# Attention stage of a three-stage kernel: one partial sum on GpSimd instead of two on TensorE, and a new order of sums, masks, hashes and weight splits

## The chip, the cores and the metric

The kernel runs on one core of a Trainium2 chip. The metric is the device time of one execution in microseconds, the median of three runs. The profile is one further execution, recorded by the hardware profiler.

## The reference

Three stages run one after the other: an attention whose mask comes from a hash, a dense layer with a gated activation and a normalisation, and a mixture of eight experts. The change touches the first stage, and the conversion of the second stage's weights, which is done during the first.

```python
def _attn_ref(q, k, v, proj):            # q, k, v: 2 x 8 heads x 768 x 64, float32
    q_bits = (einsum('bhsd,dk->bhsk', q, proj) > 0)   # 6 bits for each row
    k_bits = (einsum('bhsd,dk->bhsk', k, proj) > 0)
    mask = q_bucket[:, :, :, None] == k_bucket[:, :, None, :]
    scores = scale * matmul(q, k.T)
    scores = where(mask, scores, -1e9)
    scores = scores - max(scores, axis=-1)
    attn = exp(scores)
    attn = attn / (sum(attn, axis=-1) + 1e-09)
    return matmul(attn, v)
```

`moe_w_in` and `moe_w_out` arrive as float64, so that the kernel has to build float32 values from two 32-bit words by integer operations before it can use them.

## The kernel before

**Tiling.** The 16 heads are worked on as eight pairs j = 0..7, the two heads of a pair on partitions 0 to 63 and 64 to 127. The 768 queries of a pair are two halves i = 0, 1 of 384; the 768 keys are six blocks c = 0..5 of 128. `run` is an order written out by hand: for each half there are six steps c, each with one `score(j, i, c)` and zero to two `rowmax` calls that are nine ahead in their own list (`scan`), so that the row maxima of pair j+1 begin in the middle of pair j. After step c = 1 the function `first(j)` (for i = 0) or `second(j)` (for i = 1) is called, and it does everything else: AV of the half before, masks, hash, conversions, evacuation, sums. The reader can think of a half as a burst of scores and row maxima with a block of other TensorE work in it after step 1.

**A score.** `both` (line 220) issues four jobs of two matmuls, one for each head, in float32r: high times high, high times low, low times high, and the mask product. The result lies in a "wide" PSUM tile of two banks (`ps`, three buffers). ScalarE writes its exponential to one of eight SBUF tiles `pt` (line 260). A `rowmax` is two jobs into the same kind of PSUM tile; VectorE reduces it (line 236). So scores and row maxima share one ring of three tiles, and each tile comes free when ScalarE or VectorE has read it.

**Sums.** GpSimd adds the exponentials of two blocks each time c is odd (line 264); at c = 3 it also adds the first partial sum to the second (line 266). Two partial sums are left, one of c = 0..3 and one of c = 4, 5. `total` (line 289) adds them over partitions with a matmul by ones on TensorE in float32, into the single PSUM bank `pm`; VectorE copies the result with a small constant to `rb` (line 301). `sums` is called right after AV in `first` and `second`. For i = 1 it also sends `rb` by DMA into a small tile `rc`; `recip` (line 310), called at step c = 4 of the next pair's first half, takes the reciprocal and sends it through DRAM (`rd`) back to all partitions, and `norm` (line 321), called in `first` of the pair after, multiplies.

**AV.** `av` (line 269) is float32, twelve matmuls by the program, each of which the trace shows as two. `evac` (line 280) copies one column by VectorE (`vb`) and then the result by ScalarE.

**Masks and hash.** `hash` (line 191) is four small float32 matmuls and a VectorE threshold; `mask` (line 208) is four bfloat16 matmuls into two wide tiles and two ScalarE copies. `turn` (line 165) makes the high part of q and k on ScalarE and the low part on GpSimd.

**Weights.** The generator `Weights.steps` hands out sixteen conversions, one for each half. `convert()` in `run` calls all operations of one at once: `join` is one ScalarE and three VectorE operations in the bank `pm`; for the first eight (`w_in`) ScalarE then makes the high part and GpSimd the low part from the SBUF tile `w`, for the last eight (`w_out`) ScalarE scales in place.

**Queues.** Loads of q, k and v, the DMAs of `mr`, `rc`, `rd` and the clearing of the scratch rows (`clear`, line 1165, one of 1 MB in each of the first seven `second(j)`) all go through SP's queue in program order.

Of the kernel before, what the change touches and what calls it, by code (L numbers as in the profile page):

```python
# [8 lines left out]
F32 = mybir.dt.float32  # L9
F32R = mybir.dt.float32r  # L10
BF16 = mybir.dt.bfloat16
AF = mybir.ActivationFunctionType
ALU = mybir.AluOpType
# [3 lines left out]
P = 128  # L17
# [8 lines left out]
HW = S // 2  # L26
# [7 lines left out]
I32 = mybir.dt.int32  # L34
# [84 lines left out]
class Attention:  # L119
# [31 lines left out]
    def bank(self):  # L151
        return self.pm.tile([P, 512], F32, tag="pm", name="pm")
# [12 lines left out]
    def turn(self, j):  # L165
        nc, st = self.nc, self.st[j]
        if j == 0:
            self.hash(0)
        for nm in "qk":
            hi, lo = (self.op.tile([P, 2, HW], F32R, tag=x + nm, name=x + nm) for x in ("H", "L"))  # L170
            (nc.vector.tensor_copy if (j, nm) == (0, "q") else nc.scalar.copy)(hi, st["T" + nm])
            if (j, nm) == (0, "k"):
                self.threshold(0)
            eng = nc.gpsimd if j else nc.vector
            eng.tensor_tensor(out=lo, in0=st["T" + nm], in1=hi.bitcast(F32), op=ALU.subtract)
            st["H" + nm], st["L" + nm] = (x.rearrange("p i n -> p (i n)") for x in (hi, lo))

    def warm(self, n):
        ps = self.narrow()[:, 0:P]
# [70 lines left out]
    def score(self, j, i, c):  # L250
        nc, st = self.nc, self.st[j]
        pt = st["pt", i, c] = self.pt[self.npt % NPT]
        self.npt += 1
        ps = self.wide()
        k, q = slice(c * P, (c + 1) * P), slice(i * HW, (i + 1) * HW)
        self.both(
            ps,
            [(st[w][:, k], st[x][:, q]) for w, x in (("Hk", "Hq"), ("Hk", "Lq"), ("Lk", "Hq"), ("Fk", "Fq"))],
        )
        nc.scalar.activation(out=pt[:, :, 0:HW], in_=ps, func=AF.Exp, scale=0.125)  # L260
        if c % 2:
            acc = self.ap.tile([P, 2, HW], F32, tag="acc", name="acc", bufs=4)
            parts = st.setdefault(("acc", i), [])
            nc.gpsimd.tensor_tensor(out=acc, in0=st["pt", i, c - 1][:, :, 0:HW], in1=pt[:, :, 0:HW], op=ALU.add)  # L264
            if c == 3 and (j, i) != self.last:
                nc.gpsimd.tensor_tensor(out=acc, in0=parts.pop(), in1=acc, op=ALU.add)
            parts.append(acc)

# [11 lines left out]
    def evac(self, j, i):  # L280
        nc, st = self.nc, self.st[j]
        x = st["x", i]
        vb = self.sp.tile([P, 1], F32, tag="vb", name="vb")
        nc.vector.tensor_copy(vb, x[:, HW:HW + 1])
        if i == 0:
            st["xr"] = self.ap.tile([P, 2, HW], F32, tag="xr", name="xr", bufs=2)
        nc.scalar.activation(out=st["xr"][:, i], in_=x[:, 0:HW], func=AF.Identity, bias=vb, scale=1.0)
# [47 lines left out]
    def run(self, n, extra, fills):  # L335
        self.last = (n - 1, 1)
        scan = [(j, i, c, kh) for j in range(n) for i in range(2) for c in range(3) for kh in range(2)]

        def scans(m):
            for x in scan[:m]:  # L340
                self.rowmax(*x)
            del scan[:m]

        self.mask(0)
        next(extra)
        for _ in range(NC):
            scans(1)
            self.warm(1)
        self.submax(0, 0)
        self.load(0, "v")  # L350
        self.load(1, "v")
        for _ in range(3):
            scans(1)
            self.warm(1)
        half = [tuple(range(NC)), (0, 1, 2), (3, 4, 5)]

        def convert():
            for f in next(extra, []):
                f()

        def first(j):
            self.submax(j, 1)
            if j + 1 < n:
                self.turn(j + 1)
                self.hash(j + 1)
            convert()
            if j:
                self.av(j - 1, 1, half[0])
            if j > 1:
                self.norm(j - 2)  # L370
            if j + 1 < n:
                self.mask(j + 1)
            if j:
                self.evac(j - 1, 1)
                self.sums(j - 1, 1)
                if j + 1 < n:
                    self.load(j + 1, "v")
            if j + 2 < n:
                self.load(j + 2, "qk")

        def second(j):
            if j + 1 < n:
                self.submax(j + 1, 0)
            convert()
            self.av(j, 0, half[0])
            self.evac(j, 0)
            if j + 1 < n:
                self.sums(j, 0)
            if fills:
                fills.pop(0)()  # L390

        for j in range(n):
            for i in range(2):
                for c in range(NC):
                    self.score(j, i, c)
                    scans(((2, 1, 0, 1, 1, 1), (2, 1, 1, 1, 1, 0))[i][c])
                    if c == 1:
                        (second if i else first)(j)
                    if j and (i, c) == (0, 4):
                        self.recip(j - 1)  # L400
                    if (j, i) == self.last:
                        if c == 2:
                            self.direct(j, 0)
                            self.norm(j - 1)
                        if c == 4:
                            self.av(j, 1, half[1])
        self.av(n - 1, 1, half[2])
        self.evac(n - 1, 1)
        self.direct(n - 1, 1)
        for ops in extra:  # L410
            for f in ops:
                f()


class Weights:
# [10 lines left out]
    def steps(self, pool, bank):  # L426
        nc = self.nc
        todo = [(0, k, h) for k in range(4) for h in range(2)] + [(1, f, 0) for f in range(8)]
        wide = self.src[0].dtype != F32
# [21 lines left out]
        def convert(n):  # L451
            m, k, h = todo[n]
            w = got[n]
            ops = []
            if wide:
                H, L = w[:, :, 1], w[:, :, 0]
                w = self.wo[:, k, :] if m else pool.tile([P, 512], F32, tag="w", name="w", bufs=2)
                wi = w.bitcast(I32)
                V = nc.vector

                def join():
                    a = bank()
                    ai = a.bitcast(I32)
                    nc.scalar.activation(out=a, in_=H.bitcast(F32), func=AF.Copy, scale=2.0 ** -112)
                    V.tensor_scalar(
                        out=ai, in0=ai, scalar1=4, scalar2=1, op0=ALU.logical_shift_left, op1=ALU.logical_shift_right
                    )
                    V.scalar_tensor_tensor(
                        out=ai, in0=L, scalar=29, in1=ai, op0=ALU.logical_shift_right, op1=ALU.bitwise_or
                    )  # L470
                    V.scalar_tensor_tensor(
                        out=wi, in0=H, scalar=-(1 << 31), in1=ai, op0=ALU.bitwise_and, op1=ALU.bitwise_or
                    )

                ops = [join]
            if m:
                ops.append(lambda: nc.scalar.activation(out=w, in_=w, func=AF.Copy, scale=self.g[:, k:k + 1]))
            else:
                hi, lo = (x[:, k, h * 512:h * 512 + 512] for x in self.wi)
                ops += [  # L480
                    lambda: nc.scalar.copy(hi, w),
                    lambda: nc.gpsimd.tensor_tensor(out=lo, in0=w, in1=hi.bitcast(F32), op=ALU.subtract),
                ]
            return ops
# [3 lines left out]
        for n in range(len(todo)):  # L488
            ops = convert(n)
# [22 lines left out]
class Ffn:  # L512
# [33 lines left out]
    def split(self, i):  # L546
        nc = self.nc
        b, c = divmod(i, NC)
        st = self.st[i] = {}
        src = self.xT[:, b, :, c * P:(c + 1) * P]  # L550
        st["xh"] = self.xp.tile([P, 4, P], F32R, tag="xh", name="xh")
        st["xl"] = self.xp.tile([P, 4, P], F32R, tag="xl", name="xl")
        nc.scalar.copy(st["xh"], src)  # L553
        self.sub(nc.gpsimd, st["xl"], src, st["xh"])
# [364 lines left out]
class Experts:  # L919
# [134 lines left out]
    def finish(self, e, t):  # L1054
        nc, st = self.nc, self.st[e]
        y = self.rp.tile([P, DM], F32, tag="y", name="y")
        r = st["r"][t][:, DM:DM + 1]
        nc.vector.tensor_scalar(out=y, in0=st["o"][t], scalar1=r, scalar2=None, op0=ALU.mult)
        ins = nc.gpsimd.indirect_dma_start(
            out=self.out, out_offset=bass.IndirectOffsetOnAxis(ap=st["id"][t][:, 0:1], axis=0), in_=y, in_offset=None,  # L1060
            bounds_check=N - 1, oob_is_err=False,
        )
        apart(self.tc, "out", ins, self.C["gap"])
# [181 lines left out]
```

## Time and profile before

| | us |
|---|---|
| median of three runs | 623.01 (621.53 to 623.53) |
| the profiled execution | 620.83 |
| its span, first to last instruction of the program | 619.1 |
| TensorE busy in the span | 594.8 (96%) |
| VectorE, ScalarE, GpSimd busy | 394.1, 271.7, 317.2 |
| granted TensorE clock, mean | 0.991 |

The attention stage takes the first 248.6 us of the span, the dense layer follows to about 412 us, the experts fill the rest. Times in all rows are microseconds from the start of the span, unless a row says ns. PE is TensorE's matmul, PEld its weight load, DVE VectorE, ACT ScalarE, POOL GpSimd, SP the engine that issues most DMAs; a name with q behind it is the engine's queue. A matmul on PE is shown as busy also while it drains, so the distance from one start to the next tells more than the duration.

### The profile page before, as it was taken

To read this page: it belongs to the slowest core of one execution; us is meant where nothing else is said; L and a number is where in the kernel's file an instruction comes from. 1 tells how busy PE (TensorE), PEld (TensorE's weight loads), DVE (VectorE), ACT (ScalarE), POOL (GpSimd) and SP (SyncE) were. 2 spreads that over 40 slices of the span, in tenths; PEclk is the share of its full clock that TensorE was granted. 3 is DMA by queue.
4 is the path that set the end of the run, shared out by engine and by line. 5 is a ranking of instruction groups with operands and counts; after the bars stand their busy time and mean duration, and the time that the engine had idled before them with its cause. 6 is when DMAs were issued, how large, how long until landed. Compare 5 with 4: busy or idle time off the path is not lost.

```text
span 619.1 us, 10113 instructions
## 1 busy us (share of the span) xinstructions
PE 594.8 (96%) x3910; PEld 460.8 (74%) x3910; DVE 394.1 (64%) x788; ACT 271.7 (44%) x449; POOL 317.2 (51%) x261
## 2 busy tenths in 40 slices
PE   7979999999999999799999999989999999999994
PEld 4656666666666675578888888868899899899893
DVE  5566676767776764886777876573746645636620
ACT  2065555656555655423323322343554454553520
POOL 1076786867676546900110122052967758758731
PEclk9999999999999999989999999989999999999998
DMA  3224546163545422500000002036494494597200
GB/s 125 63 87 136 137 108 199 46 202 113 135 131 139 121 70 95 204 1 1 0 2 1 0 38 51 0 121 239 139 323 164 179 321 149 190 317 247 70 20 34
DMA packets 46229, 72.95 MB, mean 118 GB/s; under 512 B 11227, under 2 KB 20187, under 8 KB 46174
## 3 DMA queue, kind: packets, MB, share of 16 engines
q1 hardware_dynamic: 41326, 57.13, 29.3%
q10 hardware_dynamic: 2608, 8.79, 4.4%
q0 software_dynamic: 2240, 6.31, 2.9%
q8 instruction: 32, 0.52, 0.4%
q14 instruction: 23, 0.19, 0.1%
HBM read 58.39 MB, written 14.78 MB: 118 GB/s over the span
## 4 chain that ended last, share of the span: by engine, by line
PE 90%; ACT 3%; DVE 3%; issue 1%; DMA 1%; POOL 0%; POOLq 0%; SPq 0%; ACTq 0%; DVEq 0%
PE ps L224 18%; PE g L1021 15%; PE o L1043 14%; PE x L275 10%; PE h L562 10%; PE y L562 10%; PE pm L295 4%; ACT pt L260 2%; PE pm L181 2%; PE t L625 2%; PE x L988 1%; PE ps L213 1%; PE ps L195 1%; PE t L652 1%; PE lg L677 1%
## 5 line engine op out<-in xcount | busy, mean ns | idle before, releaser
L961 POOL TENSOR_TENSOR wl<-ws,wh 128x512 fp32r<-128x512 f32 x75 | 107.3, 1464 | 53.6 <-ACT wh L959 53.6
L264 POOL TENSOR_TENSOR acc<-pt,pt 128x768 f32<-128x768 f32 x48 | 87.8, 1838 | 85.5 <-ACT pt L260 85.4
L236 DVE TENSOR_REDUCE m<-ps 128x2 f32<-128x768 f32 x96 | 90.5, 957 | 43.5 <-PE ps L224 42.2
L260 ACT ACTIVATE pt<-ps 128x768 f32<-128x768 f32 x96 | 76.2, 814 | 68.2 <-PE ps L224 68.1
L959 ACT CAST wh<-ws 128x512 fp32r<-128x512 f32 x128 | 70.3, 617 | 5.2 <-POOL wl L961 3.5
L275 PE MATMUL x<-pt,v 128*64 128x385 f32 x384 | 65.8, 491 | 0.0
L961 DVE TENSOR_TENSOR wl<-ws,wh 128x512 fp32r<-128x512 f32 x53 | 57.9, 1125 | 10.3 <-ACT wh L959 10.1
L1027 DVE SCALAR_TENSOR_TENSOR hl<-g,hh 128x512 fp32r<-128x512 f32 x32 | 22.1, 692 | 59.8 <-ACT hh L1026 59.8
L538 POOL TENSOR_TENSOR xl<-xT,xh 128x512 fp32r<-128x512 f32 x12 | 16.1, 1344 | 82.4 <-ACT xh L553 38.5
L1026 ACT ACTIVATE hh<-g 128x512 fp32r<-128x512 f32 x32 | 19.2, 599 | 81.5 <-PE g L1021 81.5
L562 PE MATMUL h<-wi,xh 128*128 128x512 f32 x192 | 50.8, 408 | 3.8 <-DVE e L590 3.8
L275 PEld LDWEIGHTS x<-pt,v 128*64 128x64 f32 x384 | 26.1, 137 | 34.4 <-issue 34.0
L1043 PE MATMUL o<-wh,hh 128*128 128x512 f32 x128 | 51.1, 399 | 0.0
L1043 PE MATMUL o<-wh,hl 128*128 128x512 f32 x128 | 50.5, 394 | 0.0
L1043 PE MATMUL o<-wl,hh 128*128 128x512 f32 x128 | 50.5, 394 | 0.0
L562 PEld LDWEIGHTS h<-wi,xh 128*128 128x128 f32 x192 | 35.8, 194 | 11.9 <-issue 4.2
L562 PE MATMUL y<-wo,lh 128*128 128x512 f32 x176 | 42.7, 394 | 0.0
L224 PE MATMUL ps<-Hq,Hk 64*128 64x384 f32 x192 | 38.6, 398 | 3.1 <-ACT Fk L217 2.5
L1021 PE MATMUL g<-xh,wh 128*128 128x256 f32 x256 | 41.3, 283 | 0.3 <-ACT xh L990 0.2
L224 PE MATMUL ps<-Hk,Hq 64*128 64x384 f32 x192 | 41.5, 429 | 0.0
L1021 PE MATMUL g<-xl,wh 128*128 128x256 f32 x256 | 41.2, 282 | 0.0
L1021 PE MATMUL g<-xh,wl 128*128 128x256 f32 x256 | 40.8, 282 | 0.0
(226 smaller groups left out, 1197.0 us busy)
## 6 DMA issues: line engine op xcount, KB each, us to landing
ws<-in_moe_w_dram SPq DMA_DIRECT2D x32, 1024.0 KB, 9.8
scratch<-zero SPq DMA_DIRECT2D x7, 1030.0 KB, 7.5
r<-scratch SPq DMA_DIRECT2D x16, 257.5 KB, 4.0
raw<-in_moe_w_in_dram ACTq DMA_DIRECT2D x8, 512.0 KB, 4.0
raw<-in_moe_w_out_dram ACTq DMA_DIRECT2D x8, 512.0 KB, 4.3
q<-in_q_dram SPq DMA_DIRECT2D x8, 384.0 KB, 4.6
v<-in_v_dram SPq DMA_DIRECT2D x8, 384.0 KB, 3.0
k<-in_k_dram SPq DMA_DIRECT2D x7, 384.0 KB, 4.5
```

The lines of the kernel that those rows point to most:

```text
L224: self.nc.tensor.matmul(ps[:, h], w[r], x[r], start=(n == 0), stop=(n == len(jobs) - 1), tile_position=(D * h, 0))
L236: nc.vector.tensor_reduce(out=st["m", i][:, c, :, kh], in_=ps, axis=AX.X, op=ALU.max, negate=True)
L260: nc.scalar.activation(out=pt[:, :, 0:HW], in_=ps, func=AF.Exp, scale=0.125)
L264: nc.gpsimd.tensor_tensor(out=acc, in0=st["pt", i, c - 1][:, :, 0:HW], in1=pt[:, :, 0:HW], op=ALU.add)
L275: nc.tensor.matmul(st["x", i][D * h:D * h + D, 0:HW + 1], st["v"][:, h, c, :], st["pt", i, c][:, h, 0:HW + 1], start=(c == 0), stop=(c == ...
L295: nc.tensor.matmul(ps[D * h:D * h + D, :], C["ones"], st["acc", i][c][:, h], start=(c == 0), stop=(c == n - 1), tile_position=(0, D * h),)
L562: nc.tensor.matmul(ps, a[:, k, :], w[j](k), start=(n == 0), stop=(n == len(jobs) - 1))
L959: nc.scalar.copy(hi[:, k, :], t[:, k, :])
L961: eng.tensor_tensor(out=lo[:, k, :], in0=t[:, k, :], in1=hi[:, k, :].bitcast(F32), op=ALU.subtract)
L1021: nc.tensor.matmul(ps[:, a, :], w[:, k, f * P:(f + 1) * P], x[:, k, :], start=(n == 0), stop=(n == 11))
L1027: nc.vector.scalar_tensor_tensor(out=hl[:, 2 * g:2 * g + 2, :], in0=ps, scalar=0.0, in1=hi.bitcast(F32), op0=ALU.max, op1=ALU.subtract)
L1043: nc.tensor.matmul(st["o"][t], h[:, f, t * P:(t + 1) * P], w[:, f % 4, :], start=(f == 0 and n == 0), stop=(f == 7 and n == 2),)
```

## The change

- `score`: GpSimd adds the running partial sum at c = 5 too, so that one partial sum is left for each half (the last half of all keeps three). `total` then has two matmuls by the program instead of four.
- `sums` is called at step c = 5 of the half after, behind that step's row maxima, no longer behind AV. `recip(j-1)` moves from step 4 of the first half to step 2 of the second; `norm` stays in `first`, two pairs later, but stands behind the masks and AV; the `norm` of the last half stands at c = 5.
- `first`: AV is cut in two halves and `mask(j+1)` stands between them. `convert()` stands before `turn`.
- `hash(j+2)` runs in `second(j)`, ahead of AV, instead of `hash(j+1)` in `first(j)`; `hash(1)` stays in `first(0)`.
- `low`: the low parts are made by GpSimd in two places, k in `first`, q in `second`.
- `evac` copies `vb` by ScalarE.
- `convert()` calls one operation at step 1, and `finish()` the rest at step 3. For the eight `w_in` pieces the joined value stays in the PSUM bank; ScalarE makes the high part from it and VectorE, not GpSimd, the low part.

```diff
@@ turn
-            eng = nc.gpsimd if j else nc.vector
-            eng.tensor_tensor(out=lo, in0=st["T" + nm], in1=hi.bitcast(F32), op=ALU.subtract)
+            if j == 0:
+                self.low(0, nm, nc.vector)
+    def low(self, j, nm, eng):
+        t = self.op.tile([P, 2, HW], F32R, tag="L" + nm, name="L" + nm)
+        eng.tensor_tensor(out=..., in0=st["T" + nm]..., in1=st["H" + nm].bitcast(F32), op=ALU.subtract)
@@ score
-            if c == 3 and (j, i) != self.last:
+            if c > 1 and (j, i) != self.last:
                 nc.gpsimd.tensor_tensor(out=acc, in0=parts.pop(), in1=acc, op=ALU.add)
@@ evac
-        nc.vector.tensor_copy(vb, x[:, HW:HW + 1])
+        nc.scalar.copy(vb, x[:, HW:HW + 1])
@@ run
         def convert():
-            for f in next(extra, []):
-                f()
+            rest.extend(next(extra, []))
+            if rest:
+                rest.pop(0)()
+        def finish():
+            while rest:
+                rest.pop(0)()
         def first(j):
             self.submax(j, 1)
+            if j == 0:
+                self.hash(1)
+            convert()
             if j + 1 < n:
                 self.turn(j + 1)
-                self.hash(j + 1)
-            convert()
+                self.low(j + 1, "k", self.nc.gpsimd)
             if j:
-                self.av(j - 1, 1, half[0])
-            if j > 1:
-                self.norm(j - 2)
+                self.av(j - 1, 1, half[1])
             if j + 1 < n:
                 self.mask(j + 1)
             if j:
+                self.av(j - 1, 1, half[2])
+            if j > 1:
+                self.norm(j - 2)
+            if j:
                 self.evac(j - 1, 1)
-                self.sums(j - 1, 1)
@@ second
                 self.submax(j + 1, 0)
+                self.low(j + 1, "q", self.nc.gpsimd)
+            if j + 2 < n:
+                self.hash(j + 2)
             convert()
             self.av(j, 0, half[0])
             self.evac(j, 0)
-            if j + 1 < n:
-                self.sums(j, 0)
@@ the loop over j, i, c
-                    if j and (i, c) == (0, 4):
+                    if c == 3:
+                        finish()
+                    if c == 5 and i and j + 1 < n:
+                        self.sums(j, 0)
+                    if c == 5 and j and not i:
+                        self.sums(j - 1, 1)
+                    if j and (i, c) == (1, 2):
                         self.recip(j - 1)
                     if (j, i) == self.last:
                         if c == 2:
+                            finish()
                             self.direct(j, 0)
+                        if c == 5:
                             self.norm(j - 1)
@@ Weights.steps, convert
-                w = self.wo[:, k, :] if m else pool.tile([P, 512], F32, tag="w", name="w", bufs=2)
+                w = self.wo[:, k, :]
+                    o = w.bitcast(I32) if m else ai
+                def split():
+                    nc.scalar.copy(hi, held[0])
+                    V.tensor_tensor(out=lo, in0=held[0], in1=hi.bitcast(F32), op=ALU.subtract)
+                ops = [join] if m else [join, split]
```

## Rows read from the trace of the kernel before

**Rows 1.** The page: busy us, share of the span, instructions of each engine.
```profile
PE 594.8 (96%) x3910; PEld 460.8 (74%) x3910; DVE 394.1 (64%) x788; ACT 271.7 (44%) x449; POOL 317.2 (51%) x261
```
**Rows 2.** Busy time by stretch, attention's steady part: length, PE, PEld, DVE, ACT, POOL, PEclk.
```profile
34.00:248.00 214.00, 210.40 (x1678) 135.11 (x1679) 146.36 (x201) 122.46 (x171) 150.12 (x85) 1.00 0.44 124
```
**Rows 3.** Groups by line, PE until 300 us, and GpSimd's instructions of line 266.
```profile
L295 PE MATMUL pm<-acc,ones 128*64 128x384 f32 x132 | 24.4, 491 | 0.0
...
L266 POOL TENSOR_TENSOR acc<-acc x15: 1820/1837/1843, 42.7 to 233.9; 128x768 f32<-128x768 f32 x15
```
**Rows 4.** PE in time (start, duration, what): a first half's block, and its burst.
```profile
114.53 4.10 PE L275 MATMUL x<-pt,v 128*64 128x385 f32 x24
...
119.32 1.51 PE L295 MATMUL pm<-acc,ones 128*64 128x384 f32 x8
120.76 0.44 PE L224 MATMUL ps<-Hq,Hk 64*128 64x384 f32 x2
...
125.16 0.41 PE L224 MATMUL ps<-Hq,Hk 64*128 64x384 f32 x2
...
126.38 0.52 PE L224 MATMUL ps<-Hk,Hq 64*128 64x384 f32 x2
...
127.09 0.44 PE L224 MATMUL ps<-Hq,Hk 64*128 64x384 f32 x2
...
128.34 3.13 PE L275 MATMUL x<-pt,v 128*64 128x385 f32 x18
```
**Rows 5.** All engines in time: what reads the burst's tiles.
```profile
121.83 1.51 ACT L260 ACTIVATE pt<-ps 128x768 f32<-128x768 f32 x2 [0.30 <-PE ps L224]
...
123.78 0.81 ACT L260 ACTIVATE pt<-ps 128x768 f32<-128x768 f32 x1 [0.43 <-PE ps L224]
...
125.37 0.96 DVE L236 TENSOR_REDUCE m<-ps 128x2 f32<-128x768 f32 x1 [0.16 <-PE ps L224]
...
126.23 0.81 ACT L260 ACTIVATE pt<-ps 128x768 f32<-128x768 f32 x1 [0.51 <-PE ps L224]
```
**Rows 6.** PE in time: the block of a second half.
```profile
159.81 1.46 PE L295 MATMUL pm<-acc,ones 128*64 128x384 f32 x8
161.20 0.45 PE L224 MATMUL ps<-Hq,Hk 64*128 64x384 f32 x2
```
**Rows 7.** Groups by line, ACT from 34 to 248 us: scaling of the weights.
```profile
L477 ACT ACTIVATE wo<-wo,g 128x512 f32<-128x512 f32 x8 | 5.8, 722 | 17.8 <-DVE wo L471 17.8
```
**Rows 8.** All engines in time: the first half of pair 0, masks behind a conversion.
```profile
33.65 0.83 ACT L171 CAST Hk<-k 128x768 fp32r<-128x768 f32 x1
...
34.45 0.64 ACT L464 ACTIVATE pm<-raw 128x512 f32<-128x512 f32 x1
...
37.30 0.62 ACT L481 CAST wi<-w 128x512 fp32r<-128x512 f32 x1 [2.22 <-DVE w L471]
...
38.69 0.44 PE L224 MATMUL ps<-Hq,Hk 64*128 64x384 f32 x2 [2.51 <-ACT Fk L217]
```
**Rows 9.** VectorE's multiplication in `norm`: beside GpSimd work, and without.
```profile
118.54 2.30 DVE L325 TENSOR_TENSOR xT<-xr,rd 128x768 f32<-128x768 f32 x1
...
227.21 0.95 DVE L325 TENSOR_TENSOR xT<-xr,rd 128x768 f32<-128x768 f32 x1
```
**Rows 10.** SP's DMA issues in time; issue to landing of the clearing (line 1166).
```profile
125.24 0.33 SPq L314 DMA_DIRECT2D rd<-rc  x1
128.15 1.86 SPq L317 DMA_DIRECT2D rd<-rd  x2
...
131.41 0.70 SPq L1166 DMA_DIRECT2D scratch<-zero  x1
...
DMA to landing us min/median/max: 7.5/7.5/7.5
```
**Rows 11.** The page's DMA issues: KB, median time from issue to landing.
```profile
k<-in_k_dram SPq DMA_DIRECT2D x7, 384.0 KB, 4.5
rd<-rd SPq DMA_DIRECT2D x14, 192.0 KB, 4.3
```

More of the change, by code (lines that the diff above doesn't have):

```diff
@@ L169, in turn @@
         for nm in "qk":
-            hi, lo = (self.op.tile([P, 2, HW], F32R, tag=x + nm, name=x + nm) for x in ("H", "L"))
+            hi = self.op.tile([P, 2, HW], F32R, tag="H" + nm, name="H" + nm)
             (nc.vector.tensor_copy if (j, nm) == (0, "q") else nc.scalar.copy)(hi, st["T" + nm])
+            st["H" + nm] = hi.rearrange("p i n -> p (i n)")
             if (j, nm) == (0, "k"):
                 self.threshold(0)
-            eng = nc.gpsimd if j else nc.vector
-            eng.tensor_tensor(out=lo, in0=st["T" + nm], in1=hi.bitcast(F32), op=ALU.subtract)
-            st["H" + nm], st["L" + nm] = (x.rearrange("p i n -> p (i n)") for x in (hi, lo))
+            if j == 0:
+                self.low(0, nm, nc.vector)
+    def low(self, j, nm, eng):
+        st = self.st[j]
+        t = self.op.tile([P, 2, HW], F32R, tag="L" + nm, name="L" + nm)
+        st["L" + nm] = t.rearrange("p i n -> p (i n)")
+        eng.tensor_tensor(
+            out=st["L" + nm], in0=st["T" + nm].rearrange("p i n -> p (i n)"), in1=st["H" + nm].bitcast(F32), op=ALU.subtract
+        )
     def warm(self, n):
@@ L355, in run @@
         half = [tuple(range(NC)), (0, 1, 2), (3, 4, 5)]
+        rest = []
         def convert():
-            for f in next(extra, []):
-                f()
+            rest.extend(next(extra, []))
[4 more added lines that the diff above has]
+                rest.pop(0)()
         def first(j):
             self.submax(j, 1)
+            if j == 0:
+                self.hash(1)
+            convert()
             if j + 1 < n:
                 self.turn(j + 1)
-                self.hash(j + 1)
-            convert()
+                self.low(j + 1, "k", self.nc.gpsimd)
             if j:
-                self.av(j - 1, 1, half[0])
-            if j > 1:
-                self.norm(j - 2)
+                self.av(j - 1, 1, half[1])
             if j + 1 < n:
@@ L456, in convert @@
                 H, L = w[:, :, 1], w[:, :, 0]
-                w = self.wo[:, k, :] if m else pool.tile([P, 512], F32, tag="w", name="w", bufs=2)
-                wi = w.bitcast(I32)
+                w = self.wo[:, k, :]
                 V = nc.vector
@@ L470, in join @@
                     )
+                    o = w.bitcast(I32) if m else ai
                     V.scalar_tensor_tensor(
-                        out=wi, in0=H, scalar=-(1 << 31), in1=ai, op0=ALU.bitwise_and, op1=ALU.bitwise_or
+                        out=o, in0=H, scalar=-(1 << 31), in1=ai, op0=ALU.bitwise_and, op1=ALU.bitwise_or
                     )
-                ops = [join]
+                    held.append(a)
+                def split():
+                    hi, lo = (x[:, k, h * 512:h * 512 + 512] for x in self.wi)
+                    nc.scalar.copy(hi, held[0])
+                    V.tensor_tensor(out=lo, in0=held[0], in1=hi.bitcast(F32), op=ALU.subtract)
+                held = []
+                ops = [join] if m else [join, split]
             if m:
                 ops.append(lambda: nc.scalar.activation(out=w, in_=w, func=AF.Copy, scale=self.g[:, k:k + 1]))
-            else:
+            elif not wide:
                 hi, lo = (x[:, k, h * 512:h * 512 + 512] for x in self.wi)
```

## The prediction, made before the change was run

> **What bounds the kernel now.** I read the busy times first. TensorE is busy 96% of the span [rows 1], and in attention's steady part 210.4 of 214.0 us at a granted clock of 1.00, that is at the 2.4 GHz level [rows 2]. VectorE has 146.4, ScalarE 122.5 and GpSimd 150.1 us of work there. So a microsecond counts only if TensorE's own stream gets shorter, or if TensorE waits less.
>
> Busy is not the whole truth, so I went on to TensorE in order of time. From AV to AV a half lasts 13.81 us (114.53 to 128.34 [rows 4]), a pair about 27.6. In each half there is a block (AV, with masks and sums) and a burst of scores and row maxima. In the block the matmuls follow one another without a gap: in a first half AV, masks and sums take 6.23 us (114.53 to 120.76), of which the sums 1.44 [rows 4]; in a second half the sums take 1.39 [rows 6]. The burst is different. It is paced by the ring of three PSUM tiles: the row maximum at 126.38 could start when the reduction of 125.37 had read its tile (0.96 later, 126.33), and the score at 127.09 when the exponential of 126.23 had (0.81 later, 127.04) [rows 4, 5]. Those waits hide inside "busy". So the block is bound by TensorE's work, the burst by the latency from TensorE to ScalarE or VectorE and back. This decides what the change is worth.
>
> **The change part by part.** I sum against the profiled execution (620.83 us, its span 619.1, so 1.7 around it). It lies 2.2 below the median of 623.01; I carry the difference over to the median.
>
> *Sums, halved and moved.* The 132 instructions of `total` take 24.4 us [rows 3], 0.185 each. For 15 halves four of eight go: 60 x 0.185 = 11.1 us is what TensorE no longer has to do. But the other half does not stay where it is. Out of the block go 1.44 and 1.39 us, less about 0.10 for the switch from float32 to the scores' type, which then comes behind AV (the 24 instructions of AV take 4.10 with their drain [rows 4], so eight such are about 1.3 of the 1.39): -1.34 in a first half, -1.29 in a second. Into the burst comes an island of four such instructions, 0.65 us, and a switch on both sides. Does it fall into the burst's waits? Follow the ring in its order [rows 4, 5]. The island stands ahead of the score at 125.16. That score ends later by the island, its exponential too, and the score at 127.09 waits for that exponential whatever the row maxima between them do: what the island saves at 126.38 is paid at 127.09. So the island costs 0.65 to 0.87; I take 0.72 in first halves, where the score at 125.16 waited a little anyhow, 0.87 in second halves, where two scores stood next to each other without a switch. Per half -0.62 and -0.42. The island falls seven times into each kind of half; in the last pair, without row maxima, it costs about 0.75. Sum: 6 x -0.62 - 0.54 + 7 x -0.42 = -7.2. The ends: no wait takes in any of it (-6), or half of it vanishes in waits (-12).
> In the last half the sums of (7, 0) were an island already and lose 0.65, but GpSimd's extra addition (1.84 [rows 3]) ends about when TensorE wants it: -0.4.
>
> *GpSimd.* 15 additions of 1.84 = +27.6 us, eight low parts of weights go. Its load rises from 70% of attention to at most (150.1 + 27.6)/208 = 85%. The last addition of a half ends some 4 us into the next half, and the sums now read it at step 5, about 8 us later. Cost 0; if that cover went, TensorE would stand at the island.
>
> *Masks in the middle of AV.* No work is added; one more switch per pair, +0.05 to 0.10: +0.4. The two ScalarE copies of the masks then lie under AV's second half. In pair 0 there is no AV to hide under: the masks' copies wait behind the conversion, whose ScalarE part stands idle 2.22 us for VectorE, and the next score starts only at 38.69, 2.51 us late [rows 8]. With the conversion split, ScalarE does the 0.64 operation and two casts of 0.83 and then the masks: about 1.1 earlier, once. -1.1 (ends 0 and -2.5).
>
> *The rest of a conversion, at step 3.* It leaves the block, where AV covered ScalarE's wait (17.8 us for eight [rows 7]), and enters the burst. ScalarE has the exponentials of 121.83 to 123.34 behind one another, and the next at 123.78 [rows 5]: a gap of 0.44. The high part (0.62 [rows 8]) delays that next one by 0.18, the scaling (0.72 [rows 7]) by 0.28. The following row maximum waits for it. Three first halves of each kind: +1.4. In second halves there is room. VectorE's new low part has no row; the nearest are its operations from PSUM in the same `join`, about 0.7. It delays one reduction by about 0.7, but the island now stands ahead of the score that would wait for it: 0. Bounds: 0 and the full 0.7 in 14 halves, +9.8.
>
> *Hash one half earlier.* Its four matmuls go from a first half's block to a second's. It needs q and k, which are issued at the end of the block before: k at about 6 us after AV's start (AV and masks 4.9, two issues), and the hash is reached at about 12. k lands 4.5 after issue [rows 11]: 0, and from 1.5 us more on TensorE would wait in each of six pairs.
>
> *`vb` on ScalarE.* No row shows so small a copy there; it costs between 0 and the 0.62 of a 512-column cast [rows 8]. It lies behind AV's end, under the first score's 0.8, ahead of an exponential that starts 0.3 after that score [rows 5]. 0, at most 14 x 0.3 = +4.
>
> *`recip` and `norm`.* The reciprocal's two DMA hops now start behind the 1 MB clearing in SP's queue. Counted from AV's start in the second half: clearing issued at 3.1 (131.41 less 128.34), landed at 10.6 (7.5 later) [rows 10]. Reciprocal's DMA at about 6.8. It landed 2.9 after issue so far (125.24 to 128.15 [rows 10]); if it must wait for the clearing, at about 12. The two reads then need 0.6 + 4.3 [rows 11]: the values are there between 14.6 and 17. `norm` is reached at about 16.0 (the next AV at 12.5, plus reduction, `join` and its ScalarE operation, 3.5). It takes 2.30 beside GpSimd [rows 9], so it ends between 18.3 and 19.4. The reduction queued behind it on VectorE is wanted at 19.4 (AV and masks 4.9, two scores, a row maximum). So it just fits, or is some tenths late in the five pairs that still have reductions there: between 0 and +4, I take +1.0.
> VectorE's multiplication takes 0.95 while GpSimd rests and 2.30 while it works [rows 9]. The Trainium skill (SBUF — State Buffer, Who interferes with whom) says that a VectorE instruction with two SBUF inputs and a GpSimd instruction that reads SBUF exclude each other for a whole instruction. These rows agree. By that rule a busier GpSimd would make it up to 1.84 + 0.95 = 2.79 and the term +2 to +3 instead of +1.0.
>
> Sum: -7.2 - 0.4 + 0.4 - 1.1 + 1.4 + 1.0 = -5.9. So 620.8 - 5.9 = 614.9 for the profiled execution, and 623.0 - 5.9, about 617.0, for the median.
>
> **The rivals.**
> *The whole 11 us.* The island falls into the ring's waits, since ScalarE and VectorE catch up while TensorE does the sums. For it: both waits in the burst [rows 4, 5] are of such length. Against it: the exponential that ends the second begins only behind the island. About 14 x -0.8 = -11: 612.0.
> *The burst pays for the conversions.* The step 3 operations delay the ring by their full length: +9.8 instead of +1.4, so +2.5 in all: 625; at half of it 621. For it: the ring has no slack of its own. Against: ScalarE's gap of 0.44, VectorE's 68% load.
> *`norm` holds the reductions (slower).* If the broadcast lands 2 us later than the 17 above, VectorE stands in `norm` with every reduction behind it, the ring fills, and TensorE stops in five pairs: 5 x 2 = +10 on the forecast, 626. It outweighs the gain from about 1.2 us later than 17. For it: clearing and reciprocal share a queue. Against: the clearing is over at 10.6. The Trainium skill (DMA: Bandwidth & Descriptors, Queues, rings and completion order) says that one ring's descriptors are taken in order, which would put the reciprocal behind the clearing; no row here shows a small transfer behind one.
> *It doesn't do what it says*: the single partial sum comes too late and TensorE waits for GpSimd at the island. The slack is 8 us; I give it no chance of its own.
>
> **How the numbers follow.** Forecast 0.55 (own range 614 to 620.5), whole gain 0.20, burst pays 0.15, `norm` late 0.10. Times between 621.1 and 624.9 are within 0.3% of the median, about what a measurement here can tell from no change. Faster: forecast, whole gain and a fifth of the third: 0.78. Same: most of the third and a little of the fourth, 0.13. Slower: 0.09. The range 611.0 to 623.5 takes in the forecast, most of the whole gain and the milder half of the third case.
>
> **What would show it.** 72 instructions in `total` instead of 132; blocks of 4.9 us with masks between two AV parts; an island of 0.65 us ahead of the first score of each half, and a score three tiles later that still waits for an exponential; pairs of about 27.0 us. Wrong if the pair gets as short as 26.2 (the waits took the island in) or stays at 27.6; if VectorE idles for `rd` ahead of `norm`; if the waits of TensorE for ScalarE grow at step 3.

## The result, and the profile after

The changed kernel takes 614.70 us (median of four runs, 614.56 to 615.49) against 622.58 for the kernel before (four runs, one more than ahead of the prediction): a ratio of 0.9876, with a 95% interval of 0.9857 to 0.9896. That is 7.9 us less. In the two profiled executions the span goes from 619.1 to 612.9 us, 6.2 less; the profiled execution of before was quicker than any of its four other runs, that of after lies at its median, so the two differences don't agree to better than 2 us.

The whole difference of the traces lies in the attention stage: the dense layer's first matmul starts at 242.45 instead of 248.62, 6.17 us earlier, and what follows takes as long as it did. First the page, then busy time by stretch for attention's steady part (columns as in [rows 2]), then TensorE's group of `total` (line 303 now).

```profile
span 612.9 us, 9932 instructions
PE 586.0 (96%) x3850; PEld 454.4 (74%) x3850; DVE 389.6 (64%) x780; ACT 273.4 (45%) x465; POOL 335.6 (55%) x268
```

```profile
34.00:242.00 208.00, 202.49 (x1618) 128.29 (x1619) 141.96 (x193) 125.14 (x188) 168.32 (x92) 1.00 0.43 127
```

```profile
L303 PE MATMUL pm<-acc,ones 128*64 128x384 f32 x72 | 15.1, 507 | 0.0
```

The sums have 72 instructions where they had 132 [rows 3], and GpSimd's share of the steady part goes from 70% [rows 2] to 168.32/208 = 81%. TensorE in order of time shows the new shape: AV, masks, AV, then the burst, with the sums as an island in it.

```profile
111.63 2.16 PE L283 MATMUL x<-pt,v 128*64 128x385 f32 x12
113.72 0.82 PE L221 MATMUL ps<-bits,tab 128*128 128x384 bf16 x4
114.47 2.16 PE L283 MATMUL x<-pt,v 128*64 128x385 f32 x12
116.56 0.44 PE L232 MATMUL ps<-Hq,Hk 64*128 64x384 f32 x2
...
121.06 0.87 PE L303 MATMUL pm<-acc,ones 128*64 128x384 f32 x4
121.86 0.44 PE L232 MATMUL ps<-Hq,Hk 64*128 64x384 f32 x2
...
123.82 0.44 PE L232 MATMUL ps<-Hq,Hk 64*128 64x384 f32 x2 [0.29 <-ACT pt L268]
```

A first half's block is 116.56 - 111.63 = 4.93 us long (6.23 in [rows 4]); the island takes 0.80. The last line is the score that the prediction spoke of, two row maxima behind the island's score: it still waits for an exponential (line 268). From AV to AV a half takes 14.25 and 12.65 us in turn, 26.90 a pair; before it was 13.75 and 13.81, 27.55.

### The profile page after: what moved, and what is told of

Its sections match the earlier page's. It is cut to its first block, busy times and chain, and to the rows that moved or that the text cites. A ratio compares the mean times of both kernels' runs of the same rounds, so it can differ in the third digit from the quotient of the medians.

```text
span 612.9 us, 9932 instructions
## 1 busy us (share of the span) xinstructions
PE 586.0 (96%) x3850; PEld 454.4 (74%) x3850; DVE 389.6 (64%) x780; ACT 273.4 (45%) x465; POOL 335.6 (55%) x268
## 3 DMA queue, kind: packets, MB, share of 16 engines
q1 hardware_dynamic: 41326, 57.13, 29.1%
HBM read 58.39 MB, written 14.78 MB: 119 GB/s over the span
## 4 chain that ended last, share of the span: by engine, by line
PE 87%; ACT 4%; DVE 3%; POOL 2%; issue 1%; DMA 1%; POOLq 0%; SPq 0%; ACTq 0%; DVEq 0%
PE ps L232 16%; PE g L1055 15%; PE o L1077 15%; PE x L283 11%; PE h L596 10%; PE y L596 10%; ACT pt L268 3%; PE pm L189 2%; PE pm L303 2%; PE t L659 2%; PE x L1022 1%; POOL acc L272 1%; POOL acc L274 1%; PE ps L221 1%; PE ps L203 1%
## 5 line engine op out<-in xcount | busy, mean ns | idle before, releaser
L283 PE MATMUL x<-pt,v 128*64 128x385 f32 x384 | 67.2, 493 | 0.0
L274 POOL TENSOR_TENSOR acc<-acc 128x768 f32<-128x768 f32 x30 | 54.8, 1826 | 2.3
L232 PEld LDWEIGHTS ps<-Hq,Hk 64*128 64x128 f32 x192 | 18.2, 185 | 31.9 <-issue 13.4
```

The costliest lines, as they stand in the source:

```text
L232: self.nc.tensor.matmul(ps[:, h], w[r], x[r], start=(n == 0), stop=(n == len(jobs) - 1), tile_position=(D * h, 0))
L283: nc.tensor.matmul(st["x", i][D * h:D * h + D, 0:HW + 1], st["v"][:, h, c, :], st["pt", i, c][:, h, 0:HW + 1], start=(c == 0), stop=(c == ...
```

## Experiments

Halves are compared by the distance from the start of AV to the start of the next, since it repeats to a few hundredths of a us within one execution. "First half" is the distance from AV in a first half to AV in the second, "second half" from there on. (The hash moved from the one to the other, so the two alone are not compared between orders; pairs are.)

### Halve the sums, move nothing

```diff
-            if c == 3 and (j, i) != self.last:
+            if c > 1 and (j, i) != self.last:
```
(in the kernel before)

> The kernel before with one edit: GpSimd adds the third pair of exponentials too, the sums stay behind AV. Ring theory (work in the block counts in full, the island in the burst cost its full length too): every half loses 4 x 0.163 = 0.65 us in its block and nothing comes into the burst, so pairs of 26.25 instead of 27.55 us, 14 halves plus the sums of (7, 0): -9.7 us against before, 2 to 4 us faster than the changed kernel. Absorption theory (the burst's waits swallow part of moved work, so that moving the sums was itself a gain): this is slower than the changed kernel. GpSimd theory (its last addition ends too late for sums that stand only 5 us after the next block begins): TensorE waits at the sums for the partial sum, gain of 3 to 6 us only, pairs of 26.7 to 27.1.

Measured: 614.34 us, ratio 0.9875 (0.9856 to 0.9893): the same as the changed kernel. Second halves went from 13.75 to 13.10, exactly the 0.65 us that were expected, and the first half of pair 1 lost 0.63 (13.18). From pair 2 on first halves take 13.42 to 13.47. The trace of all engines there says why:

```profile
89.58 2.30 DVE L325 TENSOR_TENSOR xT<-xr,rd 128x768 f32<-128x768 f32 x1
...
91.10 0.44 PE L224 MATMUL ps<-Hq,Hk 64*128 64x384 f32 x2
...
91.81 0.14 DVE L284 COPY vb<-x 128x1 f32<-128x1 f32 x1
91.88 0.54 DVE L301 TENSOR_SCALAR rb<-pm 128x384 f32<-128x384 f32 x1
...
91.99 0.58 ACT L287 ACTIVATE xr<-x,vb 128x384 f32<-128x384 f32 x1 [0.25 <-DVE vb L284]
...
92.47 1.50 ACT L260 ACTIVATE pt<-ps 128x768 f32<-128x768 f32 x2
...
93.33 0.44 PE L224 MATMUL ps<-Hq,Hk 64*128 64x384 f32 x2 [0.21 <-ACT pt L260]
```

`vb` is queued on VectorE behind `norm`, ScalarE's evacuation waits for `vb`, the exponentials wait behind the evacuation, and TensorE waits for the first exponential's tile at 93.33. The block had become so short that VectorE's norm was no longer covered. The rest of the missing gain: the sums of (7, 0) cost 0.27 more rather than 0.65 less, as TensorE stands there for GpSimd's last addition (0.86 us), and the first AV comes 0.46 later than before. That last part comes with the clock: in this execution the granted clock fell to 0.5 for 3.4 us, just after TensorE had waited 2.50 us for pair 0's masks, as in [rows 8]; in the execution of before it stayed at 1.00 there. The stretch (columns as in [rows 2]):

```profile
38.96:42.38 3.42, 3.42 (x26) 3.22 (x24) 1.42 (x2) 2.09 (x3) 2.09 (x3) 0.50 0.00 0
```

So the block's work counts in full, as the ring theory says, but this kernel runs into VectorE and GpSimd in two places; the wait in pair 0 stays as a third.

### Move the sums, halve nothing

```diff
-                self.sums(j - 1, 1)            # in first
-                self.sums(j, 0)                # in second
+                    if c == 5 and i and j + 1 < n:
+                        self.sums(j, 0)
+                    if c == 5 and j and not i:
+                        self.sums(j - 1, 1)
```
(in the kernel before, with `recip` and the last `norm` moved as in the change, and five buffers for the partial sums, which are not shown)

> The kernel before with the sums moved to step 5 of the half after (reciprocal and normalisation as in the changed kernel), but with two partial sums, so eight instructions each (and five buffers for the partial sums instead of four). Ring theory: the block gets 1.34 or 1.29 us shorter, the island costs 1.30 plus 0.07 to 0.3 for its switches: +0.0 to +0.3 a half, so 0 to +4 us against before. Absorption theory: -0.5 a half, -7 us.

Measured: 629.0 us, ratio 1.012 (1.0094 to 1.0146): slower by 7 us, more than either theory gave. Second halves got 0.33 longer (14.08), near the ring theory's 0.0 to 0.3: their block lost 1.29, and their burst grew by 1.62, which is the 1.30 of the eight instructions and about 0.3 more. First halves got 1.0 longer (14.82). TensorE's waits for exponentials in the steady part were 9.9 us in the kernel before; here:

```profile
PEld ps L224 <- ACT pt L260: 21.1, 43, 1.0
```

(waits of the weight load: total, count, longest). The longest stands at the third score after a first half's block (0.94 to 0.98 us in pairs 2 to 6): ScalarE still has the two mask copies and the evacuation to do, which the sums behind the masks had covered. The prediction had no such cost in it, because the change cuts AV in two at the same time.

### Masks behind AV again

```diff
-                self.av(j - 1, 1, half[1])
+                self.av(j - 1, 1, half[0])
             if j + 1 < n:
                 self.mask(j + 1)
-            if j:
-                self.av(j - 1, 1, half[2])
```
(in the changed kernel)

> The changed kernel with the masks behind the whole of AV again, ahead of the next score. Cover theory (with the sums gone from the block nothing hides ScalarE's two mask copies, so the first exponentials of the burst come late, as in e2): +0.7 to 0.9 in each of six first halves, +4 to +6 us. Theory of the prediction (masks in the middle cost one more switch and hide nothing after pair 0): -0.4 us, no difference.

Measured: 617.52 us, ratio 0.9915 (0.9885 to 0.9944) against before, 2.8 us slower than the changed kernel. First halves take 14.87 instead of 14.25, second halves the same 12.64. ScalarE and TensorE in order of time:

```profile
117.97 0.81 ACT L225 ACTIVATE Fq<-ps 128x768 fp32r<-128x768 f32 x1
...
118.86 0.58 ACT L295 ACTIVATE xr<-x,vb 128x384 f32<-128x384 f32 x1
...
119.34 1.51 ACT L268 ACTIVATE pt<-ps 128x768 f32<-128x768 f32 x2
...
120.19 0.44 PE L232 MATMUL ps<-Hq,Hk 64*128 64x384 f32 x2 [0.68 <-ACT pt L268]
```

The copy of the second mask ends at 118.78, the evacuation follows, the exponential of a score that ended at 118.44 starts at 119.34, and the third score waits 0.68 us. So the masks in the middle of AV are the cover for the mask copies once the sums are gone. This is the cover theory of the expectation, somewhat below its sum: 0.62 a half where 0.7 to 0.9 were expected, 2.8 us in all by the medians and 3.6 by the traces where it said 4 to 6.

### Two partial sums in the islands

```diff
-            if c > 1 and (j, i) != self.last:
+            if c == 3 and (j, i) != self.last:
```
(in the changed kernel, with five buffers for the partial sums)

> The changed kernel with two partial sums again, so eight instructions in each island instead of four (and five buffers for the partial sums). If work in an island counts in full: 14 x 0.65 + 0.65 = +9.7 us, pairs of 28.2 instead of 26.9. If the burst's waits swallow part of an island: +3 to +6 us.

Measured: 622.34 us, ratio 0.9993 (0.9966 to 1.002): no faster than the kernel before. Pairs take 28.15 us instead of 26.90, so the four instructions cost 0.62 to 0.68 in a half, of 4 x 0.163 = 0.65: an island's work counts in full, nothing vanishes in the ring's waits. The attention stage is 8.9 us longer by the trace, the median 7.6.

### Conversions all at once

```diff
         def convert():
             rest.extend(next(extra, []))
-            if rest:
-                rest.pop(0)()
+            finish()
```
(in the changed kernel)

> The changed kernel, but each conversion's operations all at step 1, none at step 3. Ring theory: the six first halves with row maxima win 0.18 to 0.28 us each, pair 0 loses about 1 us again since its masks wait for the conversion: between -2 and +1 us against the changed kernel. Theory that the burst pays in full for the operations at step 3: -5 us or more against the changed kernel, pairs of 26.2 us or less.

Measured: 629.48 us, ratio 1.0123 (1.0101 to 1.0144), 14.8 us slower than the changed kernel; the expectation was between -2 and +1. Second halves are the same 12.65, first halves 15.66 to 15.79 instead of 14.25 (one of 17.44 has 3.4 us at a granted clock of 0.5 in it, and so has pair 0, where the first AV comes 2.6 later). ScalarE and TensorE in a first half:

```profile
119.28 0.65 ACT L489 ACTIVATE pm<-raw 128x512 f32<-128x512 f32 x1
...
122.22 0.59 ACT L504 CAST wi<-pm 128x512 fp32r<-128x512 f32 x1 [2.29 <-DVE pm L497]
122.70 0.83 ACT L171 CAST Hq<-q 128x768 fp32r<-128x768 f32 x1
...
123.75 0.44 PE L232 MATMUL ps<-Hq,Hk 64*128 64x384 f32 x2
...
124.87 0.81 ACT L225 ACTIVATE Fq<-ps 128x768 fp32r<-128x768 f32 x1
...
125.03 0.19 PEld L232 LDWEIGHTS ps<-Hq,Hk 64*128 64x128 f32 x2 [0.63 <-ACT Fk L225]
```

`convert()` now stands before `turn`. Undivided, ScalarE waits 2.29 us for VectorE, and the casts and the mask copies stand behind it; they end at 125.68, two us after the block. I had seen this wait in [rows 8] and costed it for pair 0 alone; with the new order it would be there in every pair. What I counted as a cost of the change (step 3) is what keeps it out.

### The scaling left out

```diff
-            if m:
-                ops.append(lambda: nc.scalar.activation(out=w, in_=w, func=AF.Copy, scale=self.g[:, k:k + 1]))
```
(in the changed kernel; not all lines are shown)

> The changed kernel without the scaling of w_out: the eight ScalarE operations at step 3 of pairs 4 to 7 are left out, so the dense layer's second matmul uses unscaled weights; everything else as it was. Theory of the prediction (an operation of 0.72 us at step 3 delays the next exponential and with it the burst of a first half by 0.28 us, nothing in a second half): first halves of pairs 4 to 6 take 0.28 us less than in the changed kernel (14.0 instead of 14.3 from AV to AV), second halves the same 12.65. If ScalarE's gaps hide it: no difference in any half. If the burst pays in full: -0.7 in both halves.

The unscaled weights send the tokens to other experts, and the branch for overfull experts runs (907 us), so only the attention stage is compared. First halves of pairs 4 and 5: 14.25 instead of 14.32; that of pair 6, which has no hash at its end, 13.43 instead of 13.52; second halves 12.60 to 12.64 instead of 12.64. So an operation of 0.72 us at step 3 costs 0.07, not 0.28. ScalarE in pair 4, the changed kernel first, then this one:

```profile
144.54 1.51 ACT L268 ACTIVATE pt<-ps 128x768 f32<-128x768 f32 x2 [0.17 <-PE ps L232]
145.94 0.72 ACT L511 ACTIVATE wo<-wo,g 128x512 f32<-128x512 f32 x1
146.55 0.81 ACT L268 ACTIVATE pt<-ps 128x768 f32<-128x768 f32 x1
```

```profile
144.54 1.51 ACT L268 ACTIVATE pt<-ps 128x768 f32<-128x768 f32 x2 [0.18 <-PE ps L232]
146.49 0.81 ACT L268 ACTIVATE pt<-ps 128x768 f32<-128x768 f32 x1 [0.43 <-PE ps L232]
```

The gap without the scaling is 0.43, as I had taken it. What I missed is that ScalarE's rows overlap: the scaling starts 0.11 before the row ahead of it ends, and the next exponential 0.11 before the scaling ends. From start to start it takes 0.61, and 0.55 were free. In pairs 1 to 3 the shorter high part stands at step 3, and their first halves take 14.24 to 14.26, as long as those of pairs 4 and 5 without any operation there.

### `vb` on VectorE again

```diff
-        nc.scalar.copy(vb, x[:, HW:HW + 1])
+        nc.vector.tensor_copy(vb, x[:, HW:HW + 1])
```
(in the changed kernel)

> The changed kernel with the one-column copy vb on VectorE again. Prediction: no difference (0), as norm and the conversion are over before AV ends. If VectorE's queue holds it up as in e1: first halves 0.2 to 0.3 us longer from pair 2 on, +1.2 us in all.

One execution: 614.85 us, but the attention stage's halves from pair 1 to 6 sum to 1.7 us more; a start that came 1.1 us earlier hides it in the total. Where `norm` takes 1.1 us the first half is 14.25 to 14.32 as in the changed kernel; where it takes 2.37 or 2.61 the half takes 15.00 and 14.78, together 1.2 more. In the changed kernel one `norm` took 2.37 too, and its half stayed at 14.24. So the copy on ScalarE is insurance against a slow `norm`, not nothing. The other 0.5 lies in two halves in which `vb` was not late (pair 1's first, pair 4's second); its cause is open.

### Clearing issued in the first half

```diff
+            if fills:                          # at the end of first
+                fills.pop(0)()
-            if fills:                          # at the end of second
-                fills.pop(0)()
```
(in the changed kernel)

> The changed kernel with the seven clearings of 1 MB issued at the end of the first half's block instead of the second's, so that the reciprocal's small DMA no longer stands behind one. If that DMA waits for the clearing in its queue: SP goes on to read it back 1.5 to 2.9 us after its issue instead of 2.1 to 4.4. Otherwise the same 2.1 to 4.4. Either way no change of the time beyond 1 us, since norm is reached later than the values land.

One execution: 614.58 us, span 612.8, as expected no change. SP's queue in time, first the changed kernel, then this one:

```profile
127.88 1.14 SPq L1200 DMA_DIRECT2D scratch<-zero  x1
132.40 0.33 SPq L322 DMA_DIRECT2D rd<-rc  x1
135.92 1.15 SPq L325 DMA_DIRECT2D rd<-rd  x2
```

```profile
131.33 0.33 SPq L322 DMA_DIRECT2D rd<-rc  x1
132.75 1.14 SPq L325 DMA_DIRECT2D rd<-rd  x2
```

SP reads the reciprocal back as soon as it has landed. Behind a clearing that took 2.15 to 4.42 us in the six cases of the changed kernel, in each of them 6.2 to 7.2 us after the clearing's issue had ended; without one it took 1.41 to 1.46 in four of six cases (2.8 and 2.9 in two, for which I have no cause). So in these rows the small transfer waits for the large one ahead of it. The Trainium skill (DMA: Bandwidth & Descriptors, Queues, rings and completion order) says that a ring's descriptors are taken in order, and these rows agree. It was over in time all the same.

### Halved sums behind AV, with the conversion in PSUM

```diff
-            if c == 3 and (j, i) != self.last:
+            if c > 1 and (j, i) != self.last:
...
-            convert()
+            if j:
+                convert()
...
                 self.mask(j + 1)
+            if j == 0:
+                convert()
...
-                ops = [join]
+                ops = [join] if m else [join, split]
```
(in the kernel before; `split` is that of the change)

> Kernel e1 (halved sums behind AV), with the conversion's low part made by VectorE from PSUM as in the changed kernel, but all of it at step 1, and pair 0's conversion behind its masks. Ring theory: -9.7 as in e1, and in pair 0 the 2.5 us wait for the masks' copies falls to about 0.7, so -1.5 to -2: about -11.5 against before, 611. GpSimd theory: GpSimd is relieved of eight low parts, so what e1 lost to it comes back in part. If VectorE's 0.7 us more in the block hold up the first reduction of a burst: +0.3 in each of the eight halves.

Measured: 619.49 us, ratio 0.9964 (0.9947 to 0.998), 5 us slower than with the halved sums alone, where 2 faster was expected. There is one `pm` bank, and `split` keeps it until VectorE has made the low part; the sums, which need the bank, start 0.7 us or more late in the seven halves that have both sums and `w_in`:

```profile
106.25 0.69 DVE L482 TENSOR_TENSOR wi<-pm,wi 128x512 fp32r<-128x512 f32 x1 [0.65 <-ACT wi L481]
...
107.08 0.87 PE L295 MATMUL pm<-acc,ones 128*64 128x384 f32 x4 [0.76 <-DVE vb L284]
```

The last row names `vb`, which the sums don't read; the low part ahead of it on VectorE ended at 106.94. In pair 0 the mask copies came early, but the conversion behind them held up the exponentials, for one of which TensorE waited 3.36 us instead. So the weight split in PSUM and the sums behind AV exclude each other: the change could do the one because it moved the other.

### Halved sums behind AV, with the three places mended

```diff
-            if c == 3 and (j, i) != self.last:
+            if c > 1 and (j, i) != self.last:
...
-        nc.vector.tensor_copy(vb, x[:, HW:HW + 1])
+        nc.scalar.copy(vb, x[:, HW:HW + 1])
...
+            if j:                              # first: pair 0 does the rest of its conversion at step 3
+                finish()
...
                         if c == 2:
-                            self.direct(j, 0)
                             self.norm(j - 1)
+                        if c == 3:
+                            self.direct(j, 0)
```
(in the kernel before, with `convert` split into `convert` and `finish` as in the change, which is not shown)

> Kernel e1 (halved sums behind AV) with three small edits: the one-column copy vb on ScalarE, since in e1 it stands behind VectorE's norm and holds up the first exponential of five bursts (first halves of 13.42 instead of 13.18 us); pair 0's conversion split, its rest at step 3, as in the changed kernel; the sums of (7, 0) one step later, since in e1 TensorE waits there for GpSimd. Cover theory (the moved sums of the change brought nothing by themselves; what e1 lacks are these three): -1.2 for vb, about -1.5 to -2.3 in pair 0, -0.7 at the end: 3 to 4 us faster than e1 and than the changed kernel, about 610.5. Rival (the order of masks, hash and sums in the changed kernel is worth something of its own): no faster than the changed kernel.

Measured: 609.67 us, ratio 0.9795 (0.977 to 0.9821): 12.7 us faster than before and 5 faster than the changed kernel. In pairs 1 to 5 second halves take 13.08 to 13.10, in pairs 1 to 6 first halves 13.17 to 13.29, which is 0.18 to 0.27 less than with the halving alone in pairs 2 to 6; from AV(7, 0) on the sums of (7, 0) cost 0.78 less than there. The wait of 2.5 us in pair 0 is gone, as ScalarE copies the masks right after the conversion's first operation:

```profile
33.95 0.64 ACT L475 ACTIVATE pm<-raw 128x512 f32<-128x512 f32 x1
...
34.53 0.79 ACT L217 ACTIVATE Fk<-ps 128x768 fp32r<-128x768 f32 x1
...
35.52 0.35 PE L224 MATMUL ps<-Hq,Hk 64*128 64x384 f32 x2
```

So halving the sums is the gain, and moving them wasn't needed for it; the three mends were not run one by one. The changed kernel's new order pays for the islands that it makes and wins back part of that by the masks and the split conversions.

## Why the prediction was right, point by point

**The total.** Forecast -5.9 (617.0), measured -6.2 by the trace and -7.9 by the medians. The range, the sign and the mechanism of the block hold; that the size agrees so well is in part luck. From the first AV to AV(7, 0) the trace is 5.05 us shorter (182.88 instead of 187.93), 4.3 without the hash of 0.78 that now stands ahead of it. The forecast for this stretch is -7.2 + 0.4 + 1.4 + 1.0 = -4.4, and of these four terms none has the measured size: the sums brought about 2 less, *Step 3* and *`norm`* cost about 2 less. Terms, by the trace:

- *Sums:* the blocks lost 1.30 and 1.29 (forecast 1.34 and 1.29). The islands cost more than 0.72 and 0.87: the two bursts grew by 0.96 and 0.99 (TensorE from the block's end to the next block, with step 3 in it). Step 3 is not the reason: where the sums were moved undivided, with nothing at step 3, the burst of a second half grew by 0.32 beyond the instructions' own 1.30. So an island costs its work and about 0.3 more, where the forecast added 0.07 and 0.22. So the term is nearer to -5 than to -7.2. The mechanism, that a burst paced by a ring of three tiles swallows nothing, is shown by the doubled islands (0.62 to 0.68 of 0.65) and by the halving in place (0.65 of 0.65).
- *Step 3:* the size was wrong: +1.4 forecast, 0.07 in each of three first halves with the scaling and nothing to be seen in the three with the high part, about 0.2 in all. The forecast let an operation delay the next exponential by its full duration less the gap; ScalarE's rows overlap. With the `norm` term this misses about as much on the other side as the islands did; the errors cancel.
- *`norm`:* +1.0 forecast, 0 measured. It took 1.1 us in five of six pairs, and no reduction waited for it. The values of `rd` landed in time although the small DMA waited for the clearing, as supposed.
- *Masks in the middle:* +0.4 forecast. The block is 0.15 longer for it (4.94 us against 4.79 for AV and masks before), 0.9 in six pairs, but without it a pair is 0.62 longer. The sentence "no work is added" was right, the cover that the step gives was named for pair 0 alone.
- *Pair 0:* -1.1 forecast. The first AV came 0.49 earlier with a hash of 0.78 ahead of it that had not stood there, 1.27 together, of which 0.34 lie in a quicker start before the first score.
- *The sums of (7, 0):* -0.4 forecast, -0.64 measured (from AV(7, 0) to the first AV of the last half, 7.35 instead of 7.99).
- *GpSimd at 81%, the hash one half earlier:* 0 forecast, and TensorE's waits for the partial sums come to 1.0 us in all, the hash shows none.
- *`vb`:* 0 forecast; against the changed kernel with it on VectorE it is worth 1.2 us in one execution, in two halves with a slow `norm`.

**The rivals.** The whole 11 us didn't come, since the islands count in full. That the burst would pay for the conversions fell with the scaling left out; a late `norm` wasn't seen. The expectation for the conversions at once failed by the same step as *Step 3*: I weighed the operations at the place where they went, and not the wait that they would have made at the place where `convert()` had moved to, ahead of the casts and the masks.

**Left open.** Why the medians differ by 1.7 us more than the spans: the starts vary (below), and the kernel before was profiled in one of its quicker executions, but no run here separates the two. Why an island costs 0.3 beside its work. What the hash's move and the low parts in two places are worth by themselves was not tried.

## What to carry to other kernels

In this kernel, removing work from a stretch that is bound by the engine's own stream gave its full length; moving it into a stretch that is paced by a ring of buffers gave nothing back, even where the engine visibly waits there, because the chain behind it is shifted by the whole length. Before a block is shortened, list what the other engines do under it: here the sums covered two mask copies, a column copy and a normalisation, and each came to light once they were gone or halved. A change of many parts is best tried part by part: the one line that halves the sums was worth all of the gain, and three small mends together brought 5 us more, which the rest of the change did not.

## What the runs showed of the hardware that I had not expected

- VectorE's multiplication with two inputs in SBUF took 1.13 us when it started shortly before a GpSimd addition ended, and GpSimd's next operation then took 2.55 instead of 1.82; where GpSimd's operation had started 0.26 us ahead, the multiplication took 2.37 and GpSimd's operation its usual 1.81. Whoever is first holds up the other; the Trainium skill (SBUF — State Buffer, Who interferes with whom) puts it as issue order deciding who blocks, and these rows agree, first the changed kernel, then the one with `vb` on VectorE. In the changed kernel `norm` came first in five of six pairs and was quicker, though GpSimd was busier. The additions alone don't do that: with the sums halved in place, GpSimd had them too, and `norm` still took 2.30 to 2.42 in five pairs behind a low part. What differs is the order of `norm` and the low parts.

```profile
114.91 1.13 DVE L333 TENSOR_TENSOR xT<-xr,rd 128x768 f32<-128x768 f32 x1
115.17 2.55 POOL L182 TENSOR_TENSOR Lk<-k,Hk 128x768 fp32r<-128x768 f32 x1
```

```profile
87.37 1.81 POOL L182 TENSOR_TENSOR Lk<-k,Hk 128x768 fp32r<-128x768 f32 x1
87.63 2.37 DVE L333 TENSOR_TENSOR xT<-xr,rd 128x768 f32<-128x768 f32 x1
```

- The granted TensorE clock stands at 0.5 (the 1.2 GHz level) from 20 us on, in which TensorE is busy without a break (10.00 of the 10 us from 20 to 30 in the changed kernel, VectorE 4.97), and rises to 1.00 (2.4 GHz) between 29.1 and 32.3 us. The first AV of kernels with the same start varies by 1.1 us with it: 44.14 where the clock rose at 29.3 (the clearing in the first half), 45.19 where it rose at 31.7 (the changed kernel). A difference of about 1 us between two single executions of this kernel can come from there.
